# Scaling and power of the q and k norms in one operation each, on three standing tiles

## The chip, the cores and the metric

The kernel runs on one core of a Trainium2 chip. The metric is the device time of one launch in microseconds, the median of three runs. One more execution was taken with the hardware profiler; its span, its times and its trace are what is read here. The engines are called PE (TensorE, with its weight loads PEld), DVE (VectorE), ACT (ScalarE), POOL (GpSimd) and SP (SyncE, which issues the loads and stores).

## The reference

Attention with normalized queries and keys, and after it a two-layer network:

```python
batch, n_heads, seq, head_dim = (8, 12, 448, 64)      # q, k, v, all float32
n_tokens, d_model, d_ff = (3584, 768, 2048)           # w_in, w_out

def rmsnorm(x, g):
    rms = np.sqrt(np.mean(x * x, axis=-1, keepdims=True) + 1e-06)
    return x / rms * g
q_n, k_n = (rmsnorm(q, g_q), rmsnorm(k, g_k))
scores = 1.0 / np.sqrt(head_dim) * np.matmul(q_n, k_n.transpose(0, 1, 3, 2))
attn = softmax(scores)            # with 1e-9 added to the sum
x = np.matmul(attn, v)            # then (B, H, S, D) -> (B * S, H * D)
...
h = x @ w_in
g = h - np.tanh(h)
return g @ w_out
```

The change concerns `rmsnorm`: for each row of 64 numbers of q and of k, the sum of squares, times 1/64 plus 1e-6, to the power -1/2.

## The kernel before

The attention is cut into 48 steps: 8 batch entries by 6 pairs of heads. A step loads q (112 partitions, 4 rows each for 2 heads, so 8 rows of 64 a partition) and k (128 partitions, 8 rows a partition) of two heads. The network works on one batch entry at a time, behind the attention of a later entry; its matmuls (line 578, and line 743 for the second layer of the first entry) come from a generator that is run in portions between the pieces of a step. Every engine's order is the order in which the Python code records its operations (`manual_schedule`); no scheduler moves them. An engine takes its instructions in that order, and one that waits holds back those behind it.

What belongs to a step s:

- `squares_of` (lines 119 and 120): ACT squares q into the tile `n` and k into the tile `sq`. There is one tile of each, shared by all steps.
- `norm_of` (lines 123 to 131), called by `norm` (line 392): a small tile `rr` of 128 x 2 x 8 numbers gets k's values in half 0 and q's in half 1. For q first and then for k: DVE sums the squares (line 129, TENSOR_REDUCE), DVE scales the sums (line 130, TENSOR_SCALAR), and POOL raises them to the power -1/2 (line 131, TENSOR_TENSOR with the operation `pow` against the constant tile `neg_half`). Each takes 8 columns, on 112 partitions for q and 128 for k.
- `norm_q` (line 397, operation at line 400): DVE multiplies q by its half of `rr` and writes the product to `n`. It waits for q's power.
- `turn` (line 406): PE transposes k (line 411) and the `n` just written (line 415), ACT copies both out as `kT` and `qT` (lines 413 and 419).
- `scores` (line 425): PE multiplies (line 438), ACT takes the exponential (line 443), with k's half of `rr` as the scale of each row.
- `totals`: PE sums the exponentials (line 510), DVE takes the reciprocal `rs` (line 515). `values` and `last_values`: PE, lines 489 and 477. `divide` (line 517): DVE multiplies the two PSUM banks of values with `rs` (line 523, four operations), which frees the banks.

The first part of the kernel is `first_slot`, nine rounds with s from -3 to 5, in which the weights are rounded besides: ACT lines 71 and 72, DVE lines 78, 79 and 82, POOL line 90, and on DVE sums of weight blocks (line 320). A round's order, as far as it matters here:

```python
scores(s + 1, 0); scores(s + 1, 1)
turn(s + 2, ...)
load(s + 4, "qk")
squares(s + 3)
norm(s + 3)
totals(s, ...)
...
last_values(s, av); values(s, av)
scores(s + 1, 2); add(s + 1); add_last(s + 1)
norm_q(s + 3)
divide(s, av)
weight(...); combine(2)
```

(The first rounds leave out what belongs to a step below 0.) On DVE a round is so: sum, scaling, sum, scaling, reciprocal, `norm_q`, four divisions, three operations of weight rounding, up to two block sums. From step 6 on the function `slot` does a step, with portions of the network's matmuls between its pieces; there `norm(s + 3)` and `norm_q(s + 3)` have such a portion between them, with the DVE work that belongs to it.

The tile `rr` of step 0 is a constant of the kernel, taken before the branch on the size of the gains; those of the other steps come from a pool with three buffers. In this run the branch takes `bounded_path`; `general_path` is in the program but is not executed.

Of the kernel before, what the change touches and what calls it, by code (L numbers as in the profile page):

```python
# [9 lines left out]
F32 = mybir.dt.float32  # L10
# [3 lines left out]
ALU = mybir.AluOpType  # L14
AX = mybir.AxisListType
# [5 lines left out]
NCH = 4  # L21
# [95 lines left out]
def squares_of(nc, sq, n, q, k):  # L117

    nc.scalar.activation(n.rearrange("p c h d -> p (c h) d"), q.rearrange("p a b d -> p (a b) d"), AF.Square)
    nc.scalar.activation(sq, k.rearrange("p a b d -> p (a b) d"), AF.Square)  # L120


def norm_of(nc, rr, sq, n, neg_half):

    D = sq.shape[2]
    for i, x in ((1, n.rearrange("p c h d -> p (c h) d")), (0, sq)):
        rows = x.shape[0]
        r = rr[:rows, i]
        nc.vector.reduce_sum(r, x, axis=AX.X)
        nc.vector.tensor_scalar(out=r, in0=r, scalar1=1.0 / D, scalar2=1e-6, op0=ALU.mult, op1=ALU.add)  # L130
        nc.gpsimd.tensor_tensor(out=r, in0=r, in1=neg_half[:rows], op=ALU.pow)  # L131


def bounded_path(tc, ctx, q, k, v, moe_w_in, moe_w_out, out, g_col, ident, ones, half_ones, neg_half, early):
# [17 lines left out]
    nc = tc.nc  # L152
    B, H, S, D = q.shape
    DFF, DM = moe_w_out.shape
    P = 128
# [19 lines left out]
    def pool(name, **kw):  # L175
        return ctx.enter_context(tc.tile_pool(name=name, **kw))
# [4 lines left out]
    small = pool("small", bufs=2)  # L181
# [205 lines left out]
    normed, turned, probs, sums, whole, xT, tt = {}, {}, {}, {}, {}, {}, {}  # L387
# [2 lines left out]
        squares_of(nc, early["sq"], early["n"], loaded["q", s], loaded["k", s])  # L390

    def norm(s):
        rr = normed[s] = small.tile([P, 2, 2 * NCH], F32, name="rr", bufs=3) if s else early["rr"]
        if s:
            norm_of(nc, rr, early["sq"], early["n"], neg_half)

# [390 lines left out]
    def first_slot(s):  # L787
# [8 lines left out]
        if s > -3:  # L796
            squares(s + 3)
        norm(s + 3)
        if has(s):
            totals(s, mm_bank())  # L800
# [291 lines left out]
def kernel(  # L1092
# [16 lines left out]
    nc = tc.nc  # L1109
    B, H, S, D = q.shape  # L1110
    P = 128
# [3 lines left out]
    consts = ctx.enter_context(tc.tile_pool(name="consts", bufs=1))  # L1115

    rows = consts.tile([P, 4 * NCH * D], F32, name="rows")
    early = {
        "q": rows[:CP, 2 * NCH * D :].rearrange("p (h c d) -> p h c d", h=2, c=NCH),
        "k": rows[:, : 2 * NCH * D].rearrange("p (c h d) -> p c h d", c=NCH, h=2),  # L1120
        "sum": rows[:, : 2 * S].rearrange("p (h s) -> p h s", h=2),
        "n": consts.tile([CP, NCH, 2, D], F32, name="n"),
        "sq": consts.tile([P, 2 * NCH, D], F32, name="sq"),
        "rr": consts.tile([P, 2, 2 * NCH], F32, name="rr"),
    }
    gcol = consts.tile([D, 2], F32, name="gcol")
    most = consts.tile([1, 1], F32, name="most")
# [2 lines left out]
    g_col = consts.tile([P, 1], F32, name="g_col")  # L1130
    ident = consts.tile([P, P], F32, name="ident")
    ones = consts.tile([P, D // 2], F32, name="ones")
    half_ones = consts.tile([P, 2, D // 2], F32, name="half_ones")
    neg_half = consts.tile([P, 2 * NCH], F32, name="neg_half")
    with tc.manual_schedule(), tc.tile_pool(name="g", bufs=1) as gp:
        grow = gp.tile([1, 2, D], F32, name="grow")
        prod = gp.tile([1, D], F32, name="prod")
        nc.scalar.dma_start(out=grow[:, 0, :], in_=g_q[None, :])
        nc.scalar.dma_start(out=grow[:, 1, :], in_=g_k[None, :])
        for name, src in (("q", q), ("k", k)):  # L1140
            fetch(nc, name, early[name], src[0, 0:2])
        for i, src in enumerate((g_q, g_k)):
            nc.sync.dma_start(out=gcol[:, i : i + 1], in_=src[:, None])
        nc.vector.memset(warm, 0.0)
        nc.scalar.activation(warm, warm, AF.Exp)
        make_identity(nc, ident)
        nc.vector.memset(neg_half, -0.5)
        nc.vector.memset(ones, 1.0)
        nc.vector.memset(half_ones, 0.0)
        for i in range(2):  # L1150
            nc.vector.memset(half_ones[i * D : (i + 1) * D, i], 1.0)
        nc.vector.tensor_tensor(out=prod, in0=grow[:, 0, :], in1=grow[:, 1, :], op=ALU.mult)
        nc.vector.tensor_tensor(out=prod, in0=prod, in1=prod, op=ALU.mult)
        nc.vector.tensor_reduce(out=most, in_=prod, op=ALU.max, axis=AX.X)
        nc.vector.tensor_scalar(
            out=flag, in0=most, scalar1=(SCORE_MAX / (scale * D)) ** 2, scalar2=None, op0=ALU.is_le
        )
        squares_of(nc, early["sq"], early["n"], early["q"], early["k"])
        norm_of(nc, early["rr"], early["sq"], early["n"], neg_half)
    bounded = nc.values_load(flag[0:1, 0:1])  # L1160

    def make_g_col():
        for base in (0, D):
            nc.vector.tensor_scalar(
                out=g_col[base : base + D], in0=gcol[:, 0:1], scalar1=gcol[:, 1:2], scalar2=scale,
                op0=ALU.mult, op1=ALU.mult,
            )
# [5 lines left out]
    with cmp.Else():  # L1173
        with ExitStack() as arm:
            make_g_col()
            general_path(tc, arm, q, k, v, moe_w_in, moe_w_out, out, g_col, ident, neg_half)


# [28 lines left out]
```

## Time and profile before

| | us |
|---|---|
| median of three runs | 1464.91 |
| lowest, highest | 1463.94, 1466.45 |
| span of the profiled execution | 1463.9 |

Busy time in the profiled execution, and what the lines of the norm take in it:

| | busy us, share | instructions |
|---|---|---|
| PE | 1429.9, 98% | 10272 |
| DVE | 818.6, 56% | 1246 |
| POOL | 512.0, 35% | 378 |
| ACT | 456.7, 31% | 850 |

| line | what | number | mean ns |
|---|---|---|---|
| 129 DVE | sum of q's squares, of k's | 48, 48 | 678, 677 |
| 130 DVE | scaling of q's sums, of k's | 48, 48 | 289, 216 |
| 131 POOL | power of q's sums, of k's | 48, 48 | 1648, 1655 |
| 400 DVE | q times its norm | 48 | 949 without the first step's, which took 693 |

The median of line 130 is 172 ns and that of line 400 is 691 ns; the means are higher because single ones took up to 1747 and 3059 ns.

How to read it: a line of the trace names the line of the program, the engine, the operation, what it writes and reads, and the shapes as partitions x elements. "Idle before" is time in which the engine stood still ahead of an instruction, with the work that released it. The page's share of busy time is a mean over stages that differ much: the first 100 us and the next 200 us, in which the weights are loaded and rounded, have another limit than the rest.

### The profile page before, as it was taken

How to read it: one execution, taken by the hardware profiler on the slowest of the kernel's cores; microseconds unless marked ns; L12 is line 12 of the kernel's file. 1: busy time of each engine (PE TensorE's matmuls, PEld its weight loads, DVE VectorE, ACT ScalarE, POOL GpSimd, SP SyncE). 2: the span in 40 equal slices, each digit the busy share in tenths (PEclk: the TensorE clock that was granted, in tenths of full speed). 3: DMA queues.
4: the chain of work that ended last, by engine and by line, in shares of the span. 5: the costliest groups of instructions: out<-in, count | busy, mean ns of one | idle time of the engine just before them, and what ended most of it. 6: DMA issues, size and time to landing. Idle time of an engine off the chain costs nothing.

```text
span 1463.9 us, 26034 instructions
## 1 busy us (share of the span) xinstructions
PE 1429.9 (98%) x10272; PEld 1187.1 (81%) x10272; DVE 818.6 (56%) x1246; ACT 456.7 (31%) x850; POOL 512.0 (35%) x378
## 2 busy tenths in 40 slices
PE   6999899999999999999999999999999999999997
PEld 3568654488888888888888888888888888889997
DVE  4999888755553665347535555555554366433322
ACT  5755443233222332223322233213322233201100
POOL 4656465224321334214422243322433133312310
PEclk9999899999999999999999999999999999999999
DMA  8769778855566545655555555555556654555663
GB/s 184 173 189 267 239 194 224 228 171 154 169 157 173 166 150 157 176 156 154 176 158 164 160 154 176 160 142 172 171 152 164 169 163 139 148 164 162 183 194 98
DMA packets 267895, 250.74 MB, mean 171 GB/s; under 512 B 164724, under 2 KB 210036, under 8 KB 267764
## 3 DMA queue, kind: packets, MB, share of 16 engines
q1 hardware_dynamic: 267760, 248.97, 60.0%
q8 instruction: 84, 1.38, 0.4%
q14 instruction: 47, 0.39, 0.1%
q10 hardware_dynamic: 4, 0.00, 0.0%
HBM read 215.48 MB, written 33.42 MB: 170 GB/s over the span
## 4 chain that ended last, share of the span: by engine, by line
PE 89%; DVE 5%; DMA 2%; SPq 1%; ACT 1%; issue 1%; POOL 0%; ACTq 0%
PE mm L578 64%; PE sc L438 9%; PE sc L489 6%; PE mm L743 4%; PE sc L477 1%; PE sc L510 1%; PE sc L411 1%; PE sc L415 1%; DMA q_nat<-in_q_dram 1%; DVE w_out L82 1%; DVE rs L515 1%; DVE w_out L78 1%; DMA gT<-in_moe_w_in_dram 1%; DVE w_out L79 1%; DVE w_out L320 1%
## 5 line engine op out<-in xcount | busy, mean ns | idle before, releaser
L578 PE MATMUL mm<-xT,w_f 128*128 128x224 f32 x1392 | 278.8, 355 | 0.0
L578 PEld LDWEIGHTS mm<-xT,w_f 128*128 128x128 f32 x1392 | 260.3, 190 | 16.9 <-issue 9.8
L578 PEld LDWEIGHTS mm<-gT,w_f 128*128 128x128 f32 x1344 | 251.4, 190 | 22.5 <-issue 15.3
L578 PE MATMUL mm<-gT,w_f 128*128 128x224 f32 x1344 | 267.7, 355 | 0.0
L131 POOL TENSOR_TENSOR rr<-rr,neg_half 112x8 f32<-112x8 f32 x96 | 156.7, 1651 | 205.1 <-DVE rr L130 203.3
L615 POOL TENSOR_TENSOR gT<-s,th 128x448 f32<-128x448 f32 x96 | 121.2, 1267 | 297.3 <-ACT th L614 296.6
L578 PE MATMUL mm<-tt,w_f 128*128 128x224 f32 x1044 | 211.2, 354 | 0.0
L578 PEld LDWEIGHTS mm<-tt,w_f 128*128 128x128 f32 x1044 | 196.1, 190 | 7.8 <-issue 7.8
L578 PE MATMUL mm<-tg,w_f 128*128 128x224 f32 x1008 | 200.4, 353 | 0.0
L578 PEld LDWEIGHTS mm<-tg,w_f 128*128 128x128 f32 x1008 | 189.5, 190 | 0.0
L438 PE MATMUL sc<-qT,kT 64*128 64x448 f32 (+1 forms) x960 | 172.6, 503 | 12.9 <-ACT p_last L443 9.2
L443 ACT ACTIVATE p<-sc,rr 128x448 f32<-128x448 f32 x192 | 106.1, 638 | 203.2 <-PE sc L438 203.2
L538 POOL TENSOR_TENSOR tt<-xT,tt 128x224 f32<-128x224 f32 x23 | 31.4, 1364 | 290.7 <-DVE xT L523 290.6
L438 PEld LDWEIGHTS sc<-qT,kT 64*128 64x128 f32 (+1 forms) x960 | 62.8, 167 | 81.4 <-issue 62.7
L515 DVE RECIPROCAL rs<-sc 128x224 f32<-128x224 f32 x42 | 65.4, 1557 | 77.5 <-PE sc L510 77.4
L443 ACT ACTIVATE p_full<-sc,rr 128x448 f32<-128x448 f32 x96 | 55.9, 632 | 144.4 <-PE sc L438 144.4
L614 ACT ACTIVATE th<-s 128x448 f32<-128x448 f32 x96 | 55.5, 578 | 101.0 <-DVE s L640 55.9
L489 PE MATMUL sc<-p,v_nat 128*32 128x224 f32 x1344 | 79.1, 353 | 0.0
L743 PE MATMUL mm<-gT,w_out 128*128 128x448 f32 x192 | 76.4, 555 | 0.0
L443 ACT ACTIVATE p_last<-sc,rr 128x224 f32<-128x224 f32 x96 | 37.9, 449 | 114.3 <-PE sc L438 114.3
L697 DVE TENSOR_TENSOR s<-mm,s 128x224 f32<-128x224 f32 x21 | 8.2, 392 | 116.7 <-PE mm L578 109.3
L523 DVE TENSOR_TENSOR xT<-sc,rs 64x224 f32<-64x224 f32 x168 | 65.3, 389 | 10.3 <-PE sc L489 2.3
(123 smaller groups left out, 1632.0 us busy)
## 6 DMA issues: line engine op xcount, KB each, us to landing
w_f<-w_in SPq DMA_DIRECT2D x196, 384.0 KB, 3.5
w_f<-w_out SPq DMA_DIRECT2D x147, 512.0 KB, 4.3
w_raw<-in_moe_w_out_dram SPq DMA_DIRECT2D x16, 768.0 KB, 5.2
out_dram<-th SPq DMA_DIRECT2D x192, 56.0 KB, 2.0
q_nat<-in_q_dram SPq DMA_DIRECT2D x47, 224.0 KB, 4.4
v_nat<-in_v_dram SPq DMA_DIRECT2D x48, 192.0 KB, 3.8
k_nat<-in_k_dram SPq DMA_DIRECT2D x94, 96.0 KB, 2.9
w_in<-w_out SPq DMA_DIRECT2D x21, 384.0 KB, 6.4
```

The costliest lines, as they stand in the source:

```text
L78: nc.vector.tensor_scalar(out=dst, in0=dst, scalar1=HI_MIN, scalar2=HI_MAX, op0=ALU.max, op1=ALU.min)
L131: nc.gpsimd.tensor_tensor(out=r, in0=r, in1=neg_half[:rows], op=ALU.pow)
L438: nc.tensor.matmul(tiles[h][i * keys : (i + 1) * keys, :n], lhsT=kT[r, c * P : c * P + keys], rhs=qT[r, i * n : (i + 1) * n], start=True, ...
L443: nc.scalar.activation(p[:, h, c if c < 2 else 0, :], tiles[h][:, :n], AF.Exp, scale=rr[:, 0, 2 * c + h : 2 * c + h + 1])
L489: nc.tensor.matmul(av[n][r : r + BL, :HS], lhsT=v_nat[:, h, c, m * BL : (m + 1) * BL], rhs=p[c][:, h, n * HS : (n + 1) * HS], start=False, ...
L515: nc.vector.reciprocal(rs, dn[:, :HS])
L523: nc.vector.tensor_tensor(out=x[m * D : (m + 1) * D, n * HS : (n + 1) * HS], in0=av[n][m * D : (m + 1) * D, :HS], in1=rs[n * D : (n + 1) * ...
L538: eng.tensor_tensor(out=t2, in0=x22, in1=t1, op=ALU.subtract)
L578: nc.tensor.matmul(bank[:, f * HS : (f + 1) * HS], lhsT=w[:, c * width + f, :], rhs=moving[p](c), start=(first and f == 0 and c == 0), sto ...
L614: nc.scalar.activation(th, h, AF.Tanh, bias=0.0, scale=1.0)
L615: eng.tensor_tensor(out=g[:, rows, cols], in0=h, in1=th, op=ALU.subtract)
L743: nc.tensor.matmul(bank[:, :S], lhsT=w_out_row(f, n // HC)[:, n % HC * P : (n % HC + 1) * P], rhs=g[:, f, :], start=(f == 0), stop=(f == C ...
```

## The change

Three things:

- `norm_of` takes the two sums (q's, then k's) one after the other, and then one scaling and one power over the whole tile `rr`, 16 columns on 128 partitions, in place of two of 8 columns each.
- The tiles `rr` are three constants of the kernel, used in turn by step number modulo 3, in place of one constant for step 0 and a pool with three buffers for the others. `neg_half` has the shape of `rr`.
- q has 112 partitions, so the last 16 of its half are never written by the sum. Before the first step POOL fills partitions 96 to 127 of q's half of each tile with 1.0, so that scaling and power find defined numbers there; nothing reads the results.

```diff
     D = sq.shape[2]
     for i, x in ((1, n.rearrange("p c h d -> p (c h) d")), (0, sq)):
-        rows = x.shape[0]
-        r = rr[:rows, i]
-        nc.vector.reduce_sum(r, x, axis=AX.X)
-        nc.vector.tensor_scalar(out=r, in0=r, scalar1=1.0 / D, scalar2=1e-6, op0=ALU.mult, op1=ALU.add)
-        nc.gpsimd.tensor_tensor(out=r, in0=r, in1=neg_half[:rows], op=ALU.pow)
+        nc.vector.reduce_sum(rr[: x.shape[0], i], x, axis=AX.X)
+    nc.vector.tensor_scalar(out=rr, in0=rr, scalar1=1.0 / D, scalar2=1e-6, op0=ALU.mult, op1=ALU.add)
+    nc.gpsimd.tensor_tensor(out=rr, in0=rr, in1=neg_half, op=ALU.pow)
...
     def norm(s):
-        rr = normed[s] = small.tile([P, 2, 2 * NCH], F32, name="rr", bufs=3) if s else early["rr"]
+        rr = normed[s] = early["rr"][s % 3]
...
-        "rr": consts.tile([P, 2, 2 * NCH], F32, name="rr"),
+        "rr": [consts.tile([P, 2, 2 * NCH], F32, name=f"rr{i}") for i in range(3)],
...
-    neg_half = consts.tile([P, 2 * NCH], F32, name="neg_half")
+    neg_half = consts.tile([P, 2, 2 * NCH], F32, name="neg_half")
...
         nc.vector.memset(neg_half, -0.5)
+        for rr in early["rr"]:
+            nc.gpsimd.memset(rr[P // 2 + P // 4 :, 1], 1.0)
...
-        norm_of(nc, early["rr"], early["sq"], early["n"], neg_half)
+        norm_of(nc, early["rr"][0], early["sq"], early["n"], neg_half)
```

`norm_of` is two lines shorter, so a line N below it is N - 2 after, up to the memsets near the end: the multiplication by q's norm at line 400 is at 398 after, the power at 131 is at 129.

## The prediction

> **What bounds the kernel now.** I began with the page's slices: TensorE is nearly full everywhere but in the first tenth or so of the span. So I asked for busy times by stage.
>
> ```profile
> 34.00:99.00 65.00, 61.45 (x714) 36.95 (x712) 61.83 (x91) 48.93 (x89) 40.42 (x26) 0.97 0.76 195
> 99.00:145.00 46.00, 45.98 (x371) 38.69 (x372) 43.90 (x60) 23.05 (x38) 26.20 (x16) 1.00 0.80 225
> 145.00:200.00 55.00, 46.61 (x308) 34.92 (x306) 47.46 (x55) 28.21 (x44) 30.40 (x18) 0.89 0.73 226
> 300.00:1320.00 1020.00, 1020.00 (x7509) 878.63 (x7508) 538.59 (x838) 290.20 (x564) 335.48 (x256) 1.00 0.56 161
> ```
>
> The columns are the stretch, its length, then busy us (and instructions) of PE, PEld, DVE, ACT and POOL, the granted clock, DMA share and GB/s. From 300 to 1320 us PE leaves nothing, and DVE is busy 53%: a change on DVE or POOL there is free unless PE comes to wait. From 34 to 99 us DVE is busy 61.83 of 65 us. The chain of waits says who sets the end there:
>
> ```profile
> 72.52 0.61 DVE rr L129
> 73.13 0.02 issue
> 73.15 0.17 DVE rr L130
> 73.33 0.60 DVE rr L129
> 73.92 0.02 issue
> 73.95 0.04 DVE rr L130
> 73.98 0.17 issue
> 74.15 1.56 DVE rs L515
> ```
>
> The pair of sums and scalings that the change touches lies on the chain itself, which stays on DVE from about 65 to 99 us. Earlier, from 34 us, the chain alternates between DVE, PE and ACT with little slack. Before 34 us it is SyncE's issues and loads of q and weights. So the first nine or so of the 48 steps decide, and I read DVE and POOL there in order of time (start, duration):
>
> ```profile
> 72.45 0.67 DVE L129 TENSOR_REDUCE rr<-n 112x8 f32<-112x512 f32 x1
> 73.15 0.17 DVE L130 TENSOR_SCALAR rr<-rr 112x8 f32<-112x8 f32 x1
> 73.23 0.68 DVE L129 TENSOR_REDUCE rr<-sq 128x8 f32<-128x512 f32 x1
> 73.95 0.17 DVE L130 TENSOR_SCALAR rr<-rr 128x8 f32<-128x8 f32 x1
> 74.15 1.56 DVE L515 RECIPROCAL rs<-mm 128x224 f32<-128x224 f32 x1
> 75.62 0.63 DVE L400 TENSOR_TENSOR n<-q_nat,rr 112x512 f32<-112x512 f32 x1
> ```
>
> ```profile
> 73.47 3.24 POOL L131 TENSOR_TENSOR rr<-rr,neg_half 112x8 f32<-112x8 f32 x2 [1.76 <-ACT w_out L71]
> 76.67 0.67 POOL L537 TENSOR_TENSOR tt<-xT 128x224 f32<-128x224 f32 x1
> 81.16 1.86 POOL L90 TENSOR_TENSOR w_out<-w_out,gT 128x768 int32<-128x768 int32 x1
> ```
>
> The reader is to see that L400, which needs q's power alone, starts at 75.62, the moment the reciprocal lets it, while POOL is still in the second power: q's ended near 73.47 + 1.62 = 75.1. The order q first, k second hides the power of q behind k's sum, k's scaling and the reciprocal, and k's power behind everything.
>
> **What the Trainium skill says.** "GPSIMD Engine Reference", 3.1 Elementwise: a two-input add takes about 2.6 cycles an element at 1.2 GHz, so 2.17 ns. The trace agrees: 0.67 us for 224 elements (L537) and 1.86 for 768 (L90) give (1.86 - 0.67) / 544 = 2.19 ns, and 0.67 - 224 x 0.00219 = 0.18 us beside. No page prices a power. "Perfetto Trace Analysis", GPSIMD Engine Instruction: time POOL by start to start rather than by the reported duration. Two powers in a row took 3.24 us, 1.62 each, which agrees with the 1.64 reported. "SBUF — State Buffer", Who interferes with whom: a tensor_scalar can need the port pair shared with GpSimd, and then waits for the whole instruction that started first. The trace agrees for L90: the L130 that started at 81.31 took 1.75 us, until L90 ended near 83.0. It does not for the power: the second L130 at 83.67 took 0.17 us inside a power begun at 83.19. "VectorE: DVE Perf Modes", The TRN2 errata — SBUF-src ops pay a fixed extra latency per instruction: a vector operation pays a fixed cost whatever its size. L130 with its 8 columns at 0.17 us fits; I take 16 columns as 0.17 too.
>
> **The change part by part.**
>
> Scaling: 96 L130 become 48. In the unblocked step above the first costs DVE 0.17 us: 73.23 - 72.45 = 0.78 from sum to sum, against 0.61 that the chain gives for a sum followed by work that needn't wait. So DVE's stream between the first sum and the reciprocal shrinks from 1.70 to 1.53 us a step.
>
> Power: two of 8 columns become one of 16, of duration X. It starts when both sums and the scaling are done. L400 now waits for all of it. Take R as the start of the first sum. Before: L400 at R + 3.17. After: sums at R and R + 0.61, scaling at R + 1.33, power at R + 1.66 (73.15 to 73.47 is 0.32 from scaling to power), end R + 1.66 + X, L400 some 0.06 later, so R + 1.72 + X. The reciprocal would let it at R + 3.00. The loss of a plain step is X - 1.45; DVE stands at L400 with L523, which frees the PSUM banks, and the weight rounding L78 to L82 behind it, and POOL's next rounding L90 waits for L82.
>
> X is not in the trace. From below: 1.64, if the power is a price per call. From above: 3.24, two calls. The nearest rows speak for a price per element: a POOL call's fixed part is 0.18 us by the fit above, so 1.64 - 0.18 = 1.46 us lies in 8 elements, and 16 give X = 0.18 + 2.92 = 3.10. That 112 and 128 partitions cost the same (1648 and 1655 ns) says that the count along the row is what can matter. I take 3.10.
>
> The six steps that do this from 31 to 86 us, each after the start of its first sum:
> - 30.96: q's sum comes 2.2 us before k's, whose load was late, so q's power was wholly done. The scaling stays at 33.86, power from 34.10, L400 at 37.26 instead of 35.40: 1.86.
> - 40.03 and 80.59: the first L130 waited for L90 (1.04 and 1.75 us). In the merged form the second sum runs under that wait and the power starts where it did (41.96, 83.19). L400 at 45.12 instead of 44.09, 86.35 instead of 85.35: 1.03 and 1.00.
> - 49.50: a wait of 0.08 for L90 also goes; power from 51.16, L400 at 54.32 instead of 52.77: 1.55.
> - 60.45 and 72.45: 3.10 - 1.45 = 1.65 each.
>
> Sum 8.74 us. Before the sum at 49.50 DVE idled 1.07 us for ACT's squares, which would swallow the 1.03 of the step before; but PE waits there for the banks that L523 frees with only some 0.3 us to spare, so I count 0.8 hidden and 7.9 left.
>
> The three steps before 31 us lose too (up to 2.5 us each at L400) but behind the loads of weights and q: ACT waits 4.4 us at 15.65 and 2.55 at 30.30 for DMA, DVE 4.66 before 30.96. I cost them at nothing. The SP queue's later q loads take a buffer freed a full step earlier by L400, and are not held.
>
> After 99 us L400 stands apart from the sums by other work, and PE is full to 145. At 187.10, on the chain, a first L130 waited 1.37 us for POOL; merged, about 0.7 of it goes. Elsewhere PE covers both.
>
> Rest: the memsets (3 on POOL, 32x8) and the wider neg_half lie before 3.5 us beside the first loads: nothing. The rr tiles rotate by three; the exps that read the tile three steps back were issued a step or more earlier, so no new wait.
>
> Total 7.9 - 0.7 = +7.2 us on the profiled span of 1463.9. The runs' median is 1464.91, 1.0 above that span, so 1472.1.
>
> **The rivals.**
>
> A price per call: X = 1.64. The steps give 0.40, -0.43, 0.09, 0.19, 0.19, -0.46: zero; with the 0.7 at 187 it is 1464.2, no change. For it: nothing but that the operation is small; against it the 0.18 us fixed part of the other POOL calls.
>
> Faster: the same X, and POOL's 1.6 us freed in each step also shortens the port waits of DVE from 145 to 200 us, where the chain is on DVE: L400 took 2.33 us at 148.88 and 2.02 at 194.79, against 0.63 undisturbed. Both gone is 3.1, with 0.7 makes 3.8: 1461.1. It decides only where X is below 1.9 or so; beyond, the early loss outweighs it. Against it: order of start decides such waits, and they may fall elsewhere.
>
> A part of both: a set-up within the power and a smaller price per element, X about 2.3: some 0.8 less a step, 1467.5.
>
> Stalls in the full stage: DVE stands up to 2 us longer at L400 in some 32 later steps, and PE waits for a bank. At 0.5 us each that is 16 more: 1488. Against it: L400 at 611.02 is followed by a transpose, and the next eviction there comes only at 619.57.
>
> That the edit doesn't do what it says I rule out: the program has one scaling and one power a step.
>
> **How the numbers follow.** Price per element 0.66, 1472.1; with X from 2.6 to 3.24, the hidden 0.8 counted or not, 1469 to 1474.5. Part of both 0.12, 1465.5 to 1469. Per call 0.12, 1463 to 1465.5. Faster 0.07, 1460 to 1462. Stalls 0.03. Within 0.2%, 2.9 us, is about what a measurement of this kernel can tell from no change: 1462.0 to 1467.8. Slower: 0.66 + 0.03 + 0.03 of the mixed case = 0.72; the same 0.21; faster 0.07. The range 1465.5 to 1475.5 takes in the first two cases.
>
> **What would show it.** The POOL row of the power: 48 of 128x16, near 3100 ns if I am right, near 1650 if the call is the price. DVE's idle time at L400 put down to that row: 8.5 us in 9 now, above 15 then, most of it between 35 and 86 us. The first L578 of the steady stage some 7 us later, and 300 us after it unchanged in pace. If the power is under 2.3 us, or DVE's waits show in the early stage but the first L578 is no later, the prediction is wrong.

## The result, and the profile after

| | us |
|---|---|
| before, median of 4 runs | 1464.43 (1462.94 to 1466.45) |
| after, median of 4 runs | 1471.70 (1469.57 to 1472.88) |
| ratio, with its 95% interval | 1.0047 (1.0030 to 1.0065) |
| span of the profiled execution, before and after | 1463.9, 1469.9 |

The kernel is 7.3 us slower by the medians; the two profiled spans are 6.0 apart. The working below is against the spans.

Busy time by stage of the kernel after (stretch, length, then busy us and instructions of PE, PEld, DVE, ACT and POOL, granted clock, DMA share, GB/s):

```profile
34.00:99.00 65.00, 56.54 (x668) 29.78 (x668) 52.96 (x78) 43.24 (x80) 35.62 (x19) 0.92 0.76 190
99.00:145.00 46.00, 45.04 (x370) 37.41 (x369) 44.05 (x56) 25.38 (x42) 23.95 (x13) 1.00 0.66 170
145.00:200.00 55.00, 48.95 (x334) 40.27 (x333) 45.42 (x58) 25.00 (x40) 28.83 (x16) 0.91 0.77 241
300.00:1320.00 1020.00, 1020.00 (x7457) 880.07 (x7456) 538.75 (x803) 292.06 (x569) 323.85 (x222) 1.00 0.56 162
```

From 34 to 99 us DVE, which was busy 61.83 of 65 us before, is now busy 52.96: it stands. From 300 us on nothing has changed. The chain of waits of the kernel after, in the same stage, shows what it stands for:

```profile
65.15 1.20 DVE rr L127 x2
66.35 0.02 issue
66.37 0.19 DVE rr L128
66.56 0.02 issue
66.58 0.02 POOLq L129
66.60 0.09 issue
66.69 2.91 POOL rr L129
69.60 0.02 issue
69.62 0.04 DVE n L398
69.66 1.03 issue
70.69 0.37 DVE xT L521
```

Before, the chain stayed on DVE at this place: sums, scalings, reciprocal. Now it goes through GpSimd's power for 2.91 us. One step of DVE, and POOL beside it, in order of time (start, duration; in brackets the idle time before, and what ended it):

```profile
78.98 0.67 DVE L127 TENSOR_REDUCE rr<-n 112x8 f32<-112x512 f32 x1
79.57 0.67 DVE L127 TENSOR_REDUCE rr<-sq 128x8 f32<-128x512 f32 x1
80.28 0.17 DVE L128 TENSOR_SCALAR rr<-rr 128x16 f32<-128x16 f32 x1
80.48 1.56 DVE L513 RECIPROCAL rs<-mm 128x224 f32<-128x224 f32 x1
83.53 1.13 DVE L398 TENSOR_TENSOR n<-q_nat,rr 112x512 f32<-112x512 f32 x1 [1.49 <-POOL rr L129]
84.58 1.62 DVE L521 TENSOR_TENSOR xT<-mm,rs 64x224 f32<-64x224 f32 x4
```

```profile
80.59 2.90 POOL L129 TENSOR_TENSOR rr<-rr,neg_half 128x16 f32<-128x16 f32 x1 [2.36 <-ACT p_full L441]
83.46 0.65 POOL L535 TENSOR_TENSOR tt<-xT 128x224 f32<-128x224 f32 x1
```

This is the step that the prediction showed at 72.45 us. The multiplication L398 comes 4.55 us after the first sum, where it came 3.17 us after it. It idles 1.49 us for the power, and takes 1.13 us where it took 0.63: POOL starts its subtraction L535 the moment the power ends, and L398 ends 0.55 us after that subtraction. The page's rows of the power and of the multiplication, as counts, busy us, mean ns and idle time before:

```profile
L129 POOL TENSOR_TENSOR rr<-rr,neg_half 128x16 f32<-128x16 f32 x48 | 140.0, 2917 | 227.6 <-DVE rr L128 224.5
L398 DVE TENSOR_TENSOR n<-q_nat,rr 112x512 f32<-112x512 f32 x47 | 49.2, 1047 | 69.0 <-POOL rr L129 58.1
```

The rest is read from a few marks in time: the first sums of some steps, and DVE's first eviction of the network's first layer (L634 before, L632 after), called the first eviction from here on.

| us | before | after | difference |
|---|---|---|---|
| first sum of the fourth step | 30.96 | 30.75 | -0.21 |
| first eviction | 98.36 | 107.58 | +9.22 |
| first sum near 190 | 187.02 | 196.76 | +9.74 |
| first sum of the step after it | 223.17 | 229.01 | +5.84 |
| first sum near 290 | 286.94 | 293.21 | +6.27 |
| span | 1463.9 | 1469.9 | +6.0 |

So 9.2 us are lost by 108 us, 3.9 come back in one step between 187 and 223 us, and the rest passes through the full stage, 6.3 us at its start and 6.0 at the end.

### The profile page after: what moved, and what is told of

Same layout as the page of the kernel before. It is cut to its first block, busy times and chain, and to the rows that moved or that the text cites. A ratio compares the mean times of both kernels' runs of the same rounds, so it can differ in the third digit from the quotient of the medians.

```text
span 1469.9 us, 25944 instructions
## 1 busy us (share of the span) xinstructions
PE 1429.8 (97%) x10272; PEld 1185.5 (81%) x10272; DVE 816.0 (56%) x1198; ACT 456.2 (31%) x850; POOL 496.5 (34%) x333
## 4 chain that ended last, share of the span: by engine, by line
PE 92%; DVE 2%; DMA 2%; SPq 2%; ACT 1%; POOL 1%; issue 1%; ACTq 0%; POOLq 0%
PE mm L576 66%; PE sc L436 9%; PE sc L487 6%; PE mm L741 5%; PE sc L508 2%; PE sc L475 1%; PE sc L413 1%; PE sc L409 1%; DMA w_raw<-in_moe_w_out_dram 1%; POOL rr L129 1%; PE mm L487 0%; SPq L114 0%; DMA gT<-in_moe_w_in_dram 0%; DMA k_nat<-in_k_dram 0%; PE mm L508 0%
## 5 line engine op out<-in xcount | busy, mean ns | idle before, releaser
L129 POOL TENSOR_TENSOR rr<-rr,neg_half 128x16 f32<-128x16 f32 x48 | 140.0, 2917 | 227.6 <-DVE rr L128 224.5
L513 DVE RECIPROCAL rs<-sc 128x224 f32<-128x224 f32 x42 | 65.4, 1557 | 77.5 <-PE sc L508 77.4
L398 DVE TENSOR_TENSOR n<-q_nat,rr 112x512 f32<-112x512 f32 x47 | 49.2, 1047 | 69.0 <-POOL rr L129 58.1
L521 DVE TENSOR_TENSOR xT<-sc,rs 64x224 f32<-64x224 f32 x168 | 65.3, 388 | 10.2 <-PE sc L487 2.2
```

Source lines behind the costliest of these rows:

```text
L129: nc.gpsimd.tensor_tensor(out=rr, in0=rr, in1=neg_half, op=ALU.pow)
L398: nc.vector.tensor_tensor(out=n.rearrange("p c h d -> p h c d"), in0=t, in1=rr[:CP, 1].rearrange("p (h c) -> p h c", h=2)[:, :, :, None].t ...
L513: nc.vector.reciprocal(rs, dn[:, :HS])
L521: nc.vector.tensor_tensor(out=x[m * D : (m + 1) * D, n * HS : (n + 1) * HS], in0=av[n][m * D : (m + 1) * D, :HS], in1=rs[n * D : (n + 1) * ...
```

## The experiments

The marks of every profiled execution, from here on called by the name of the run. "Length near 40" and "length near 190" are the times from the first sum near 40 us, and near 190 us, to the next step's. "Halved" is for how long the granted clock of PE was half of full speed around that step (from 33 to 43 us, and from 195 to 212 us), in us.

| run | halved near 40 | length near 40 | first eviction | halved near 200 | length near 190 | span | median of all its runs |
|---|---|---|---|---|---|---|---|
| before | 0 | 9.47 | 98.36 | 3.4 | 36.15 | 1463.9 | 1464.43 |
| before, again | 0 | 9.47 | 98.31 | 3.4 | 36.22 | 1464.2 | one run, 1466.0 |
| before, with powers at its end | 6.8 | 12.08 | 100.57 | 3.4 | 36.22 | not comparable | one run |
| after | 3.4 | 11.10 | 107.58 | 0 | 32.25 | 1469.9 | 1471.70 |
| one scaling, two powers | 0 | 9.76 | 100.45 | 6.8 | 38.67 | 1469.8 | 1470.95 |
| two scalings, one power | 3.4 | 11.34 | 109.44 | 0 | 33.05 | 1474.2 | 1474.31 |
| merged from the tenth step on | 0 | 9.47 | 98.80 | 0 | 32.26 | 1460.2 | 1463.03 |
| merged up to the ninth step | 0 | 9.73 | 107.28 | 3.4 | 36.22 | 1471.1 | 1473.25 |
| after, divisions first | 3.4 | 12.88 | 102.27 | 0 | 32.26 | 1464.8 | 1465.76 |
| before, divisions first | 3.4 | 12.47 | 102.26 | 0 | 34.56 | 1466.2 | 1467.71 |
| no scaling on DVE | 6.8 | 12.11 | 99.33 | 0 | 32.60 | 1461.0 | 1461.24 |
| one scaling from the tenth step on, two powers | 6.8 | 12.11 | 101.11 | 6.8 | 38.89 | 1470.3 | 1469.23 |
| after, gaps of PE filled | 0 | 9.73 | 107.28 | 0 | 32.25 | 1467.6 | 1469.03 |
| no scaling on DVE, one power from the tenth step on | 6.8 | 12.08 | 100.33 | 0 | 32.09 | 1461.5 | 1461.79 |

The third row is the kernel before as well: what that run adds stands at the end of the program, from 1454.5 us on, and everything ahead of it is the same. So the kernel before has three profiles, and they differ: where the clock was halved near 40 us, that step took 2.6 us longer and the first eviction came 2.2 us later. Over all the runs the step takes 9.47 to 9.76 us without a halved clock and 11.10 to 12.88 with one. First evictions are thus best compared between runs that agree in the first column.

The kernel before was timed beside each of them on the same chip. Its median was 1464.43 us beside the kernel after (4 runs), 1463.08 beside the next four runs of the table (19 runs), 1462.90 beside divisions first, no scaling and one scaling late (51 runs), and 1463.17 beside the last two (24 runs). Ratios below are against these. Against the larger sets the kernel after would be 8.5 to 8.8 us slower, not 7.3.

### Scaling alone and power alone

```diff
+    # after, with the powers apart again
+    for i, rows in ((1, n.shape[0]), (0, sq.shape[0])):
+        nc.gpsimd.tensor_tensor(out=rr[:rows, i], in0=rr[:rows, i], in1=neg_half[:rows, i], op=ALU.pow)
-    nc.gpsimd.tensor_tensor(out=rr, in0=rr, in1=neg_half, op=ALU.pow)
```

> The changed kernel with the power undone: sums of q and k, one scaling of 16 columns, then two powers of 8 columns, q's first. Theory (the length of the 16-column power, 2.90 us against 1.64, is what L400 of before, here L399, waits for): q's power ends 1.64 us after the scaling, so L399 starts 3.36 us after the first sum instead of 3.17 in a plain step, 0.4 later in the step whose k came late, 0.45 earlier in the two steps in which a scaling waited for POOL: zero in sum, 1463.5 to 1465.5. Rival (the wait for k's sum and the joint scaling costs, not the power): most of the 7 us stays, 1469 to 1472.

```diff
+        # after, with the scalings apart again
+        nc.vector.tensor_scalar(out=r, in0=r, scalar1=1.0 / D, scalar2=1e-6, op0=ALU.mult, op1=ALU.add)
-    nc.vector.tensor_scalar(out=rr, in0=rr, scalar1=1.0 / D, scalar2=1e-6, op0=ALU.mult, op1=ALU.add)
     nc.gpsimd.tensor_tensor(out=rr, in0=rr, in1=neg_half, op=ALU.pow)
```

> The changed kernel with the scaling undone: sum, scaling, sum, scaling as before, then one power of 16 columns on the standing tiles. Theory: L399 waits for the 2.90 us power as in the changed kernel, and the power starts 0.17 us later in a plain step and up to 0.75 later where the first scaling waits for POOL: 1472 to 1474.5, slower than the changed kernel by 0.5 to 2.5. Rival (the joint scaling is the cost): 1463 to 1466.

Measured: scaling alone 1470.95 us (1469.29 to 1471.87), ratio 1.0048 (1.0034 to 1.0062); power alone 1474.31 us (1470.83 to 1476.07), ratio 1.0067 (1.0050 to 1.0084). The power alone came as the theory has it. The scaling alone did not: it was to be free and costs 7.9 us. Its profile tells that this is another loss than the one of the merged power. At the first eviction it is only 2.1 us behind. It is 2.8 behind in the step near 190 us, and that step is 2.5 us longer than before's. There q's multiplication (L399 in this run, L400 before) took 5.08 us, where before's took 2.02, and PE's clock was halved for 6.8 us in place of 3.4. Whether the early steps or the merged scaling itself bring that about is asked below.

### The early steps alone, the later ones alone

`norm_of` got an argument that chooses between the form of before and the form of after; the three standing tiles are there in all steps.

```diff
-            norm_of(nc, rr, early["sq"], early["n"], neg_half)
+            norm_of(nc, rr, early["sq"], early["n"], neg_half, s > 8)   # the other run: s <= 8
```

> Steps 0 to 8 (the rounds in which weights are rounded) scale and raise q and k apart as before, steps 9 to 47 together as in the changed kernel; standing tiles everywhere. Theory: the loss is made in the early rounds alone, and the 3.4 us that the changed kernel won back between 108 and 300 us were a delay swallowed there, not a gain of the merged form: 1463.5 to 1466. First rival (the standing tiles, or stalls of the later steps, cost): 1469 to 1472. Second rival (the merged form gains in the later rounds by shorter port waits): 1460.5 to 1462.5.

> Steps 0 to 8 together, steps 9 to 47 apart as before. Theory: the whole loss and its partial recovery are here: 1470.5 to 1473. First rival (later steps cost): 1464 to 1466. Second rival (the recovery was the merged form's gain in the later rounds): 1473.5 to 1475, since it is then missing.

Measured: merged from the tenth step on 1463.03 us (1460.04 to 1466.04), ratio 0.9999 (0.9987 to 1.0011); merged up to the ninth 1473.25 us (1470.52 to 1475.91), ratio 1.0067 (1.0049 to 1.0084). The loss lies in the first nine steps, and 39 merged steps with the standing tiles cost nothing. The profiles also place the 3.9 us that came back: the length near 190 is 32.26 us where the late steps are merged and 36.22 where they are apart, whatever the early steps do. What makes that difference can be read in the kernel before (three lines of DVE and one of PE) and in the kernel after (three lines of DVE):

```profile
187.74 1.37 DVE L130 TENSOR_SCALAR rr<-rr 112x8 f32<-112x8 f32 x1
192.05 2.29 DVE L82 SCALAR_TENSOR_TENSOR w_out<-w_raw,w_out 128x768 int32<-128x768 int32 x1
194.79 2.02 DVE L400 TENSOR_TENSOR n<-q_nat,rr 112x512 f32<-112x512 f32 x1
198.33 1.12 PE L411 MATMUL sc<-ident,k_nat 128*128 128x128 f32 x4 [2.28 <-DVE rs L515]
```

```profile
198.07 0.78 DVE L128 TENSOR_SCALAR rr<-rr 128x16 f32<-128x16 f32 x1
201.00 0.96 DVE L82 SCALAR_TENSOR_TENSOR w_out<-w_raw,w_out 128x768 int32<-128x768 int32 x1
202.41 1.09 DVE L398 TENSOR_TENSOR n<-q_nat,rr 112x512 f32<-112x512 f32 x1
```

DVE comes to the reciprocal (L515, L513 after) 3.05 us sooner after its first sum: 0.78 are won at the scaling, 1.33 at the rounding L82 and 0.93 at the multiplication. PE does not stand before it any more, for 2.28 us, and the halved clock that followed this stand before is gone too. Here are the two stretches of 3.40 us around the end of the stand, in the kernel before (columns as above):

```profile
194.80:198.20 3.40, 1.25 (x4) 0.34 (x2) 3.40 (x3) 2.15 (x3) 3.40 (x3) 1.00 0.32 29
198.20:201.60 3.40, 3.27 (x11) 2.45 (x12) 3.29 (x6) 2.00 (x4) 1.32 (x2) 0.51 0.94 323
```

The kernel before with divisions first, below, tells the two apart: PE stood 2.30 us at the same place, no halved clock followed, and the step took 34.56 us. Of the 3.9 us, some 2.3 are then the stand and 1.6 the halved clock.

The timed runs do not follow that to the end. The late form's profiled span is 3.7 us below before's, its median equals before's. Before's first two profiled executions took 1465.69 and 1466.0 us, 2.6 and 2.9 above its median in these sets; the late form's took 1462.08, 1.0 below its own. How much of the 3.9 us a usual execution gains is therefore left open; 1471.7 against 1473.25 for the kernel with the early steps alone merged points to part of it, and those intervals overlap.

### The divisions ahead of the multiplication

In the early steps the four divisions by the softmax sums (L521, four instructions of 1.6 us in all) stand behind the multiplication. They need nothing of the power. The first run puts them ahead in the changed kernel, the second in the kernel before.

```diff
     def first_slot(s):
...
+        if has(s):
+            divide(s, av)
         norm_q(s + 3)
         if s == -3:
             early["g_col"]()
-        if has(s):
-            divide(s, av)
```

> The changed kernel; in the early steps q's multiplication (L398) is issued after the four divisions (L521) and not ahead of them, so that VectorE divides while GpSimd takes the power. Theory (the early loss is VectorE standing at L398 for the longer power with the divisions queued behind): the four divisions take 1.6 us, about what the wait lasted, so the step is as long as in the kernel before: first eviction at 97 to 100 us and 1461 to 1466 us in all. Rival (the loss is not that standing but the longer occupation of GpSimd, or a port): first eviction still at 105 to 108 us, 1469 to 1473 us.

> The kernel before with the same reordering, as control: there q's power ends before the reciprocal does, so VectorE does not stand at its multiplication in most steps. Theory: little changes, first eviction 96 to 99 us, 1461 to 1465 us. Rival (the reordering gains by itself, for instance because the divisions no longer wait behind the multiplication's port): first eviction 93 to 96 us, 1457 to 1461 us; then what the run of the changed kernel with this order shows has to be read against this one.

Measured: the changed kernel 1465.76 us (1462.18 to 1466.69), ratio 1.0011 (1.0002 to 1.0019); the kernel before 1467.71 us (1464.73 to 1470.55), ratio 1.0028 (1.0015 to 1.0041). Neither first eviction came where it was expected: 102.27 and 102.26. But they are equal. With the divisions first, the longer power costs nothing by then, where it cost 9.2 us; and the clock was halved for 3.4 us near 40 in both. DVE in the changed kernel with this order, the step that answers to the one above:

```profile
76.70 0.67 DVE L127 TENSOR_REDUCE rr<-n 112x8 f32<-112x512 f32 x1
77.29 0.67 DVE L127 TENSOR_REDUCE rr<-sq 128x8 f32<-128x512 f32 x1
78.00 0.17 DVE L128 TENSOR_SCALAR rr<-rr 128x16 f32<-128x16 f32 x1
78.20 1.56 DVE L513 RECIPROCAL rs<-mm 128x224 f32<-128x224 f32 x1
79.87 1.63 DVE L521 TENSOR_TENSOR xT<-mm,rs 64x224 f32<-64x224 f32 x4
81.53 0.86 DVE L398 TENSOR_TENSOR n<-q_nat,rr 112x512 f32<-112x512 f32 x1
```

DVE doesn't stand at all. The multiplication starts 4.83 us after the first sum, later than in the kernel after (4.55), and 5 us of time are won all the same: for the early steps it counted less when q is multiplied than what stood behind it. From the sum near 50 us on the steps are nearly back at before's length: from one first sum to the next 10.94, 12.22 and 8.36 us, where before took 10.95, 12.00 and 8.14, and after 12.30, 13.91 and 10.01.

What is lost with this order lies in the step near 40, as the control shows: of the 3.9 us between 98.36 and 102.26 it has 3.0 (12.47 us against 9.47). PE now stands for `n`, here in the kernel before with divisions first, and the clock is halved from 37.5 us on:

```profile
37.90 0.98 PE L415 MATMUL sc<-ident,n 112*128 112x112 f32 x4 [1.91 <-DVE n L400]
```

The third profile of the kernel before has nearly the same step, 12.08 us, with a halved clock and without that stand. So the price of the order is for the most part a halved clock in one step, which the stand for `n` may have brought about, but which the kernel before can have without it. My expectation of "about as before" for both had forgotten PE's transposes behind the multiplication.

### One scaling, only in the later steps

```diff
-            norm_of(nc, rr, early["sq"], early["n"], neg_half)
+            norm_of(nc, rr, early["sq"], early["n"], neg_half, s > 8)   # one scaling, two powers
```

> One scaling for both and two powers of 8 columns as in the run with the scaling alone merged, but only from the tenth step on (after 113 us); the steps up to there as in the kernel before. Theory (the loss of that run between 140 and 200 us was a wait of q's multiplication for the port behind GpSimd's other work, a matter of when the steps fall and not of the merged scaling): with the early steps unchanged 1462 to 1466.5 us. Rival (the merged scaling itself, by which q's power starts after k's sum, costs in that stage): the 3.7 us that the run lost after 108 us come back, 1466.5 to 1469 us.

Measured: 1469.23 us (1467.52 to 1472.08), ratio 1.0042 (1.0027 to 1.0057): beyond the rival's end, far from the theory's. The merged scaling with two powers costs in the later steps too, with the early steps of the kernel before. POOL and then DVE of this run (L135 is the power, L619 the subtraction of the network's tanh, L90 the rounding of weights, L404 the multiplication):

```profile
192.72 3.54 POOL L135 TENSOR_TENSOR rr<-rr,neg_half 112x8 f32<-112x8 f32 x2
196.23 1.34 POOL L619 TENSOR_TENSOR gT<-s,th 128x448 f32<-128x448 f32 x1
197.53 1.84 POOL L90 TENSOR_TENSOR w_out<-w_out,w_raw 128x768 int32<-128x768 int32 x1
199.34 2.21 POOL L619 TENSOR_TENSOR gT<-s,th 128x448 f32<-128x448 f32 x2
```

```profile
197.03 5.07 DVE L404 TENSOR_TENSOR n<-q_nat,rr 112x512 f32<-112x512 f32 x1
```

The multiplication reads two tiles of SBUF. It was issued while POOL was in L619, and finished 0.5 us after POOL's run of four instructions had ended. The chain of waits goes through it in the run with the scaling alone, as 5.00 us at 196.38. So the 5 us are, as far as the trace tells, a wait of DVE behind POOL's other work; PE stands 4.05 us behind it, and its clock is halved for 6.8 us. In the kernel before the two powers were over at 192.4, L90 stood alone, and the same multiplication took 2.02 us; with one power (after, and power alone) 1.09 and 1.10.

At the first eviction this run is 2.7 us behind before's first profile, though its early steps are those of before, as are those of the run merged from the tenth step on, which evicted at 98.80. That is the halved clock near 40 again: PE stood 2.17 us up to 33.75, then ran at half clock from 34.9 to 41.7, and the step took 12.11 us, as in the third profile of the kernel before (12.08). So of the 6.4 us in this run's span only some 3.6 belong to the later steps.

### PE's gaps filled

In the kernel after, PE stood 1.74 us ahead of q's transposes at 38.18, and the granted clock then was half for 3.4 us (columns as in the stages above):

```profile
34.50:37.90 3.40, 1.76 (x9) 0.71 (x6) 1.78 (x2) 3.40 (x7) 2.81 (x1) 1.00 0.86 176
37.90:41.30 3.40, 3.12 (x28) 1.85 (x32) 3.22 (x8) 2.88 (x6) 0.00 (x0) 0.50 0.29 80
```

The same followed its stands of 2.06 us at 68.8 and 2.05 at 82.8, but not one of 2.00 us that ended at 25.72. The prediction knew nothing of that, so it was tried whether the loss is partly the clock's.

```diff
+        for i in range(fill):                            # 10 in three early steps
+            nc.tensor.transpose(tq[:, :P], kn[:, i % NCH].rearrange("p h d -> p (h d)"), ident)
         for c in range(NCH):
             nc.tensor.transpose(
                 tq[:, c * CP : (c + 1) * CP], n[:, c].rearrange("p h d -> p (h d)"), ident[:CP, :CP]
```

> The changed kernel with ten idle transposes (1.65 us at the 0.165 us of a transpose, overwritten at once by the real ones) ahead of the transposes of q (L413) in the three early steps where the trace of the changed kernel shows TensorE standing 1.74, 2.06 and 2.05 us there and then running 4 to 6 us at a granted clock near 0.5. Theory (the halved clock after such a stand is part of the early loss, in the step from 41.67 to 52.77 us above all): no halved clock at 36 to 42 us, that step 10.0 to 10.5 us long instead of 11.1, first eviction at 105 to 107 us instead of 107.6, and 1469 to 1471.3 us in all. Rival (TensorE at half clock is not what the steps wait for): first eviction at 107.3 to 109 us, 1471 to 1473.5 us.

Measured: 1469.03 us (1468.74 to 1469.41), ratio 1.0039 (1.0028 to 1.0051). No halved clock is left between 22 and 108 us, and the step from 41.53 us took 9.73 us, against 11.10. So far the theory. But the first eviction came at 107.28, as the rival has it: the step after it took 13.53 us, against 12.30. There ACT's squares now waited for k's load:

```profile
50.55 0.68 ACT L119 ACTIVATE n<-q_nat 112x512 f32<-112x512 f32 x1
52.42 0.63 ACT L120 ACTIVATE sq<-k_nat 128x512 f32<-128x512 f32 x1 [1.19 <-DMA k_nat<-in_k_dram]
```

The halved clock cost 1.4 us in one step, and the load of k would have cost nearly as much without it. The run merged up to the ninth step says the same: no halved clock near 40, and the first eviction at 107.28. So the halved clock is not the cause of the kernel after's early loss. It does bear on its size, since two of before's profiles have none near 40: against the third, which has it, the loss at the first eviction is 7.0 us and not 9.2. From the sum near 50 us to the first eviction the three profiles of before agree, 48.8 to 48.9 us, and the kernel after takes 54.8. These 6.0 us do not hang on the clock: it was halved twice more in that stretch of the kernel after, and with the gaps filled the two steps concerned took 13.90 and 10.02 us without it, against 13.91 and 10.01.

The 94 timed runs of the kernel before in the three larger sets bear this out. Their spans go from 1458.3 to 1467.4 us, and they follow the mean granted clock: the median is 1464.0 us in the 35 runs with 0.990 or less, and 1459.1 in the 28 with 0.993 or more. The four runs of the kernel after had 0.989 to 0.992, and their spans lie 5.9 to 7.4 us above the medians of before's runs at the same clock.

Of the 2.3 us that the span with filled gaps gains on the kernel after, 0.3 arise before 108 us. Of the rest, 0.9 lie in the step from 152 us, where the clock was halved for 6.8 us in place of 10.2, and 1.2 in the step from 228 us, where PE stood 1.24 us for an exponential in place of 2.47. The two programs are the same there; why the stands differ is open.

"TensorE: Matmul & The Clock Gate" of the Trainium skill (What's actually happening) says that PE falls to half clock after an idle window of about 3.4 us, and that these windows run freely. The length agrees: in all these traces a halved clock lasts 3.41 us, or two or three times that, if the start and the end of a trace are left out. But the window need not be idle throughout. In the kernel after PE worked for 1.76, 1.28 and 1.30 us of the 3.40 us ahead of the three halved stretches. That windows run freely would explain why a stand of 2.28 us near 198 us was followed by a halved clock in the kernel before (PE busy for 1.25 of 3.40 us) and one of 2.30 us was not with divisions first (2.02 of 3.40 us, from 198.0 on).

### The price of a power

The kernel before, with powers of seven widths at its end, three of each, and nothing beside them.

> The kernel before, and at its end, with nothing beside them, GpSimd powers of 1, 2, 4, 8, 16, 32 and 64 columns on 128 partitions, three times each; its time in all says nothing. Theory (a price per column): 158 ns a column and 0.38 us beside, from the 1.64 us of 8 and the 2.90 us of 16 columns: 0.54, 0.69, 1.01, 1.64, 2.90, 5.4 and 10.5 us. Rival (a price per group of columns, or a large fixed part): the short ones at 1.2 to 1.6 us all alike, or steps at some width.

The rows of that line, one for each shape (counts, busy us, mean ns):

```profile
L867 POOL TENSOR_TENSOR gT<-gT 128x64 f32<-128x64 f32 x3 | 31.6, 10547 | 0.2
L867 POOL TENSOR_TENSOR gT<-gT 128x32 f32<-128x32 f32 x3 | 16.3, 5428 | 0.2
L867 POOL TENSOR_TENSOR gT<-gT 128x16 f32<-128x16 f32 x3 | 8.7, 2901 | 0.2
L867 POOL TENSOR_TENSOR gT<-gT 128x8 f32<-128x8 f32 x3 | 4.9, 1637 | 0.2
L867 POOL TENSOR_TENSOR gT<-gT 128x1 f32<-128x1 f32 x3 | 1.7, 551 | 0.2
```

From 1 to 64 columns it is (10547 - 551) / 63 = 159 ns a column, and 0.39 us beside. As expected: the call has no price that merging could save but 0.39 us.

### The kernel before once more

> The kernel before once more, for a second profile of it. Theory (what the first 100 us and q's multiplication in the stage from 140 to 240 us take repeats from one execution to the next): first eviction at 98 to 99.5 us, q's multiplication near 195 us 2.0 us long, the step after 187 us 36 us long. Rival (these waits are a matter of chance): first eviction up to 3 us off, or the step after 187 us shorter than 34 us.

The first eviction at 98.31, the multiplication near 195 us 2.02 us long and the length near 190 of 36.22 us repeat the first profile within 0.1 us, as the theory has it. But these two executions happen to agree. The run with the powers at its end, the same kernel up to there, has the sum near 50 us 2.3 us later. Here are the 6.8 us ahead of the difference, first in before's first profile and then in that run, and the sum that follows in it:

```profile
33.40:40.20 6.80, 6.49 (x82) 3.52 (x86) 6.30 (x12) 6.80 (x14) 2.11 (x3) 1.00 0.79 176
33.30:40.10 6.80, 6.80 (x34) 3.94 (x38) 6.34 (x12) 6.80 (x13) 2.38 (x3) 0.50 0.77 181
```

```profile
51.81 0.69 DVE L129 TENSOR_REDUCE rr<-n 112x8 f32<-112x512 f32 x1 [3.65 <-ACT n L119]
```

At half clock PE did 34 instructions where it had done 82, and DVE idled 3.65 us for ACT's squares where it had idled 1.07. So the rival was right in part: a first eviction can be off by 2 us with no change of the program. The multiplication near 195 us and the length near 190 are the same in all three.

### No scaling at all

If an early step is bound by DVE, taking the scaling away should gain. ACT squares x/8, and each row of squares has a 65th element of 1e-6, so that the sum is the mean plus 1e-6; powers are two, as before.

```diff
-    nc.scalar.activation(sq, k.rearrange("p a b d -> p (a b) d"), AF.Square)
+    nc.scalar.activation(sq[:, :, :D], k.rearrange("p a b d -> p (a b) d"), AF.Square, scale=float(D) ** -0.5)
...
-        nc.vector.tensor_scalar(out=r, in0=r, scalar1=1.0 / D, scalar2=1e-6, op0=ALU.mult, op1=ALU.add)
...
+        nc.vector.memset(early["n"][:, :, :1], 1e-6)
+        nc.vector.memset(early["n"][:, :, 1 + 2 * D :], 1e-6)
+        nc.vector.memset(early["sq"][:, :, D:], 1e-6)
```

> The kernel before without any scaling on VectorE: ScalarE squares x/8 and each row of 64 squares has a 65th element of 1e-6, so the sums are mean plus 1e-6 at once; powers are two of 8 columns as before. Theory: an early step loses two scalings of 0.17 us and the waits of L130 for GpSimd's port (0.87 and 1.58 us in two of them), so the first eviction comes 2 to 4.5 us earlier (94 to 96.5 us) and the end at 1459 to 1463 us. Rival (what is gained early is given back by 300 us, as part of the loss was): first eviction earlier, the time 1463 to 1465.5 us.

The last run takes one power in place of two from the tenth step on.

> The kernel without scaling on VectorE, with one power of 16 columns for both norms from the tenth step on (after 113 us) and two of 8 columns before. Theory (the longer power costs only in the early steps, and where one power stood in place of two the step from 187 us on was 3 to 4 us shorter): 1459 to 1462 us, at or below the 1461.2 of the kernel without scaling. Rival (that kernel's step of 32.6 us there has the gain already): 1461 to 1463.5 us.

Measured: 1461.24 us (1458.95 to 1464.37), ratio 0.9989 (0.9980 to 0.9998); with one power late 1461.79 us (1459.91 to 1464.88), ratio 0.9988 (0.9980 to 0.9996). Both are 0.1% faster than the kernel before, inside what was named as no change, and about 10 us faster than the changed kernel. The first evictions came at 99.33 and 100.33, not at 94 to 96.5. Both runs had the halved clock near 40, which the expectation knew nothing of; against the profile of before that had it too (100.57) they are 1.2 and 0.2 us ahead. The gain that was expected of a step shows behind it: from the sum near 50 us on the steps take 10.48, 11.62 and 7.74 us (the second run 10.48, 11.63 and 7.75), where before took 10.95, 12.00 and 8.14. The profiles gain near 190 us besides (32.60 and 32.09 against 36.15). The second tells nothing between its theory and its rival, since its time lies in both.

## Why the prediction was right

The time was 1471.7 us, where 1472.1 had been forecast, and the mechanism is the one named: a power priced by the element, DVE standing at q's multiplication with the divisions behind it, in the steps before 100 us. The runs with the early steps alone, with the later ones alone, and with the divisions first show it. That the sum came within 0.4 us is in part luck (the profiled span rose by 6.0 us, where 7.2 had been forecast): two of its terms were off, one by some 1.3 us and one by 3.2, in opposite directions, and the kernel before by itself moves by several us from run to run.

**Where the bound is.** Right. From 300 to 1320 us PE is full in both kernels, and the 39 later steps merged cost nothing.

**The power, X.** 2.90 us, not 3.10. Dividing all of 1.64 - 0.18 us by 8 was the error: the fixed part is 0.39 us, not the 0.18 of an addition. The rival of a price per call falls, and so does the one of a large set-up.

**The six steps.** Losses by the prediction, the same with X = 2.90, and as the growth of the time from one step's first sum to the next (the last to the first eviction):

| step at (before) | predicted | with 2.90 | measured |
|---|---|---|---|
| 30.96 | 1.86 | 1.66 | 1.85 |
| 40.03 | 1.03, of which 0.8 hidden | 0.83, of which 0.8 hidden | 1.63 |
| 49.50 | 1.55 | 1.35 | 1.35 |
| 60.45 | 1.65 | 1.45 | 1.91 |
| 72.45 | 1.65 | 1.45 | 1.87 |
| 80.59 | 1.00 | 0.80 | 0.82 |
| sum | 7.9 | 6.7 | 9.4 |

The first mis-sized term is "so I count 0.8 hidden". DVE's idle time ahead of the sum at 49.50 was 1.07 us, and it grew to 1.47. Filling PE's gap shows what takes turns there: without the halved clock most of the 0.83 was hidden in that step (growth 0.26), and then more was lost in the next behind k's load. A further 0.5 us in each of the steps at 60.45 and 72.45 is by the trace a wait for POOL, and so for the shared port, that was not foreseen: L398 now starts together with POOL's L535, since both follow the power. Of the 2.7 us between 6.7 and 9.4 the step at 40.03 has 1.6 (the 0.8 that wasn't hidden, and 0.8 more that goes with the halved clock or, without it, with k's load), the two port waits have 0.9, and 0.2 is that the first of the six steps began 0.21 us earlier. The 1.6 holds against the two profiles of before whose clock was full there. Against the third the step at 40 is 1.0 us shorter after, and the sum is 7.2: where both have the halved clock, the delay is hidden there, and more of it than was foreseen. The prediction took no account of the clock at all.

**The first three steps** were to be hidden behind loads. Right: their multiplications came 2.56, 4.41 and 1.33 us later, the second more than the 2.5 that was named, and the sum of the fourth step began at 30.75 against 30.96 all the same.

**The later gain.** 0.7 us was counted at 187.10 for a scaling that waits for POOL. It came there: the scaling took 0.78 us where it had taken 1.37, and the work behind it came 0.78 sooner. But 3.9 came back by 223 us in the profiled execution. Two more waits behind POOL shortened in the same step, at L82 and at the multiplication, a stand of PE of 2.28 us went with them, and a halved clock with that. The length near 190 is 32.1 to 33.1 us in the six runs with one power there, and 36.2 in four of the five with the form of before; the fifth, with the stand and without the halved clock, has 34.6. That one power is needed for it is not shown, since the run without scaling had 32.6 with two. This is the second mis-sized term. It is near the "Faster" rival's idea, that POOL's freed time shortens the port waits, at one of the two places where that rival put it: 2.02 us of the multiplication became 1.09. At the other, the 2.33 us at 148.88, nothing changed (2.33 at 158.09).

**What would show it.** The power's row and the unchanged pace after 300 us came as named. DVE's idle time at L398 for the power is 61.2 us in 33 places in the trace, above the 15 that were named, but "most of it between 35 and 86 us" was wrong: from 25 to 100 us it is 12.1 us. 45 of the rest lie after 300 us, where PE is full, and cost nothing. The first L578 of the steady stage was 6.25 us later (293.97 to 300.22), not 7.

**The change's other part.** The prediction took the merged scaling for a small gain, 0.17 us a step. With one power it is one, if anything (1471.7 against 1474.31, with overlapping intervals). With two powers it cost 7.9 and 6.3 us in two runs (some 2.7 of the second profile's are a halved clock near 40), in good part through the multiplication meeting POOL's other work, with q's power starting after k's sum as a likely reason; that nothing of it was foreseen didn't matter only because the change merges both. That q loads are not held was right; that k's load can be what a step waits for was not considered.

## What to carry to other kernels

Merging two instructions saves their fixed parts and gives up that the first result is there early: here 0.39 us of 3.28 saved, and 1.4 us more wait for whoever needed the first half. Before merging, look at who stands behind the instruction that consumes the first half, on its own in-order engine; moving independent work ahead of the wait can pay for it, as the divisions did, until the moved consumer itself is needed. A local idle gap hides a delay only if the engines that end the gap don't depend on the delayed one. And before a difference of two or three us at one mark is put down to a change, compare the granted clock of the stretch ahead of it: the kernel before differs that much from itself.

## What the runs showed of the hardware

- A power on GpSimd takes 159 ns a column on 128 partitions beside 0.39 us, linear from 1 to 64 columns, against 2.19 ns for an element of an addition.
- A VectorE multiplication of two SBUF tiles can stand behind several GpSimd instructions in a row: 5.07 us, for what takes 0.63 alone. "SBUF — State Buffer" of the Trainium skill (Who interferes with whom) says that such an instruction contends with a GpSimd instruction that reads SBUF, and for the two-port modes that the first to issue has the ports for its whole instruction. The contention is there; but the waiting one did not get its turn when the instruction ahead of it ended: three more of POOL's went first.
- TensorE's granted clock fell to half for 3.41 us, or two or three times that, behind stretches of 3.4 us in which TensorE worked for about half the time or less: 1.76, 1.28 and 1.30 of 3.40 us in the kernel after. Stands of nearly equal length (2.28 and 2.30 us) were followed by it in one run and not in another. In one step of one and the same program it made 12.08 us of 9.47; where the step waited for a load without it (the kernel after, gaps filled), its loss was down to 0.3 us by the end of the next step.
